# Three element-wise steps of an attention normalisation placed on GpSimd instead of two of them on VectorE, with another set of planner keys

## The chip, the cores and the metric

The kernel runs on one core of a Trainium2 chip. The metric is the device time of one execution in microseconds (us). Lower is better. Before the change three runs took 578.23, 578.06 and 575.93 us, a median of 578.06 us. The profiled execution is another one and took 579.15 us.

The engines are named as the profile names them: PE is TensorE's matmul, PEld its weight load, DVE is VectorE, ACT is ScalarE, POOL is GpSimd, SP is SyncE, which issues the DMAs.

## What is computed

A token-wise gate mixes two branches of the same input x (2048 tokens of 640 features):

```python
g = sigmoid((x * gate_w).sum(-1))
out = g * A(x) + (1 - g) * B(x)
```

Branch A is causal attention in four segments of 512 tokens with 32 heads of size 20, plus a linear memory that is carried from segment to segment. What is touched by the change is how its two parts are put together:

```python
for s in range(4):                                   # segments
    p = softmax(qs @ ks.T * scale + mask)
    a_dot = p @ vs
    num = phi(qs) @ M
    den = phi(qs) @ z + 1e-6
    a_mem = num / den
    o = g * a_mem + (1 - g) * a_dot                  # g = sigmoid(beta), one number for each head
    M, z = M + phi(ks).T @ vs, z + phi(ks).sum(rows)
```

The heads' outputs go through a 640x640 product with wo. Branch B picks the single token with the highest router score, sends it through a gated feed-forward net, and adds the result to that token alone.

## The kernel before

Work is cut into 32 groups n = 0 to 31, each of four heads of one segment. The heads are done in two halves; inside a half the segments s = 0 to 3 follow each other. For each of the eight (half, segment) units the kernel projects q, k and v on TensorE (each fp32 product as three passes on a high and a low part, line 704), writes the split q and k through DRAM and fetches them back in another layout, and then works through four groups.

One group has these steps. `a_step` (line 907) makes logits in five pieces on TensorE and VectorE reduces each to row maxima (lines 928 and 933). `maxima` (line 937) transposes these maxima and sends them into the rows of q by two small DMAs. `b_step` (line 960) makes the logits again, transposed, with the maximum taken off, ScalarE takes the exponential (line 975), and GpSimd zeroes the part above the diagonal (line 977). `pv_step` (line 983) multiplies by v (line 998); the v operand has a column of ones, so that the row sum of the softmax comes out as a 21st column. VectorE transposes that result into the first plane of a tile `nt` (line 1002). For segments 1 to 3, `memory_read` (line 845) has put phi(q) times the memory into the second plane of the same tile (lines 854 and 857), and GpSimd added 1e-6 to its denominators (line 859).

`norm` (line 1005) follows. VectorE takes the reciprocals of both denominators into a small tile `zr` (line 1012) and multiplies them by the gates (line 1013). It then multiplies the attention plane by its reciprocals (line 1017). Where s is above 0, GpSimd multiplies the memory plane by its own (line 1019) and VectorE adds the two planes (line 1020). Finally VectorE transposes the sum into a tile `on` (line 1021), of which there is only one, and a DMA writes it to DRAM. At the very end the heads' outputs are read back from DRAM, split into high and low parts (`o_load`, line 1195) and multiplied by wo (`o_job`, line 1216).

The order of all instructions on all engines is written out before the program is built, by a planner (`Plan.order`, line 207). Every task has an engine, an estimated duration, its dependences and a key. The planner steps through an imagined time, and at each step gives an engine the ready task with the lowest key. The keys are in units of one group: `n + PV` is the key of group n's last product, for example, and the constants at lines 51 to 69 set how far ahead of or behind its group each sort of task is wanted. The planner keeps two special rules: VectorE tasks that read two operands in SBUF (`lazy`) are not started while GpSimd is busy in the imagined time, and GpSimd tasks are not started while such a VectorE task runs (lines 246 to 249). Each engine then runs its list in that order, and waits where a dependence is not met.

A product that has been accumulated over one pair of row groups continues over the other pair only behind a "poke": VectorE copies two numbers out of the bank (line 692) and TensorE waits for that copy.

Of the kernel before, what the change touches and what calls it, by code (L numbers as in the profile page):

```python
# [14 lines left out]
OP = mybir.AluOpType  # L15
# [32 lines left out]
)  # L48
QTILE = {0: 0, 1: 1, 2: 3, 3: 4}
OFF = {0: 0, 1: 32, 2: 16, 3: 48}  # L50
LEAD = 3.1467
FIRST, UP, DOWN, DSTEP, FLOAD = 15.289, 0.1308, 19.6553, 0.2292, 0.944
LATER = 0.2501
PATIENCE = -0.3274
SHY = 2.468
EAGER = 1.4585
NEAR, FAR = 0.009, 0.0208
FETCH, XLOAD, XSPLIT = 1.3841, -0.8162, 1.0739
HALF, HSTEP, HLOAD, HALFV, HVSTEP = 0.0598, 0.099, 0.1226, 1.522, 0.1321
COPY, PHI, KEYS = 1.2662, 0.5548, 0.4812  # L60
MREAD, MWRITE, MSTEP = 0.7209, 1.594, 0.2955
PV, ASTEP, TOP, TURN, EXPS = 1.1417, 1.089, 0.738, 0.1362, 2.4648
WOAT, WOSTEP, OAT, OSTEP, OJOB, OLOAD = -0.4104, 0.1942, 0.9554, 0.0415, 0.1035, 0.4306
SLACK, GRACE = 0.1324, 0.1102
LASTO, LASTJ = 1.1526, 2.4243
WEIGHT = {"P1": 7.7099, "P2": 6.6659, "T4": 4.3409, "V0": 3.394, "V1": 7.0074}
PTS = 8
WARM = 13
POKE = 1.7235


ASTEPS = (([(0, 3, 0, 512)], 384, 1, 128), ([(0, 2, 0, 384), (0, 0, 384, 128)], 256, 2, 128),
# [14 lines left out]
def sub(ap, off, dims):  # L87
    return bass.AP(tensor=ap.tensor, offset=ap.offset + off, ap=[list(ap.ap[0])] + dims)
# [47 lines left out]
class Plan:  # L136
# [70 lines left out]
    def order(self):  # L207
# [24 lines left out]
        def choose(e):  # L232
# [44 lines left out]
            if e == "PE":  # L277
# [14 lines left out]
                def rank(c):  # L292
                    est, t = c
                    k = t.key
                    if t.opens is not None and t.opens.kind in DRAIN:
                        x = late[DRAIN[t.opens.kind]] - (est + t.dur + 0.3) - PATIENCE
                        k += SHY * x if x > 0 else EAGER * max(x, -1.0)
                    return k, t.seq
# [101 lines left out]
def tile_infini_mod(  # L400
# [12 lines left out]
    nc = tc.nc  # L413
# [27 lines left out]
    def dma(key, dst, src, reads, writes, desc, wide=16, issue=Plan.ISSUE, extra=0.0, kind="x"):  # L441
        kind = "in" if not reads else "out" if not writes else kind
        plan.add("SP", issue, lambda: nc.sync.dma_start(dst, src), key, reads, writes, desc=(*desc, wide, extra, kind))

    def dve(key, dur, fn, reads, writes, alone=None):
        n = sum(not isinstance(x[0] if isinstance(x, tuple) else x, Ps) for x in reads)
        plan.add("DVE", dur, fn, key, reads, writes, lazy=n > 1 and n == len(reads) if alone is None else alone)
# [4 lines left out]
    def pool(key, dur, fn, reads, writes):  # L452
        plan.add("POOL", dur, fn, key, reads, writes)

    def pe(key, dur, fn, reads, writes, mode="R", opens=None, lazy=False, fence=None):
        return plan.add("PE", dur, fn, key, reads, writes, mode=mode, opens=opens, lazy=lazy, fence=fence)
# [10 lines left out]
    def stream(n):  # L467
        return max(n * 0.000447 + 0.003, 0.11)
# [216 lines left out]
    def paired(ps, steps, operands, n, key_of, reads_of, kind):  # L685

        total, last, phase = len(steps), None, steps[0][1]
        for i, (k, ph) in enumerate(steps):
            fence = None
            if ph != phase:  # L690
                phase = ph
                poke = plan.add("DVE", 0.16, lambda: nc.vector.tensor_copy(nil.t, banks[ps.pair][0:1, :, 0:1]),  # L692
                                key_of(i) - POKE, poked=last)
                fence = (last, poke)
# [3 lines left out]
            def fn(i=i, k=k, ph=ph, ends=ends):  # L698
                t = banks[ps.pair]
                for p in range(3):  # L700
                    for r in range(2):
# [3 lines left out]
                                         start=i == 0 and p == 0, stop=ends and p == 2, skip_group_check=True)  # L705
            last = pe(key_of(i) + (LATER if kind != "O" else 0.0), 3 * stream(n) + 0.01, fn, reads_of(k), [ps], opens=ps if i == 0 else None, fence=fence)

# [275 lines left out]
    def pv_step(n, key):  # L983
        u, g = divmod(n, 4)
        ps = Ps("pv", 1)
        pos = (g + 2) % 4
        v = va[u % 2]
        assert now["v", u % 2, 0] == now["v", u % 2, 1] == u
        pt = {(p, c): pts.pop((n, p, c)) for p in range(2) for c in range(4)}

        def fn():
            o = banks[ps.pair]
            for c in range(4):
                w = L - 128 * c
                for j in range(4):
                    h = 4 * pos + j
                    t, to, pitch = pt[j % 2, c]
                    nc.tensor.matmul(o[32 * j:32 * j + 32, ps.bank, L - w:], v.t[:, c, VW * h:VW * h + 32],  # L998
                                     sub(t.t, 512 * (j // 2) + to, [[pitch, 4 - c], [1, 128]]), start=c == 0, stop=c == 3)
        pe(key, 2.2, fn, [*dict.fromkeys(t for t, *_ in pt.values()), v], [ps], mode="C", opens=ps)  # L1000
        nt = nts.pop(n) if n in nts else nt_ring.take()
        dve(key, 0.72, lambda: nc.vector.transpose(nt.t[:, 0, :], banks[ps.pair][:, ps.bank, :]), [ps], [(nt, 0)])  # L1002
        norm(n, nt, key)

    def norm(n, nt, key):

        u, g = divmod(n, 4)
        hf, s = divmod(u, SEG)
        z, o = zr_ring.take(), on_ring.take()
        i = 2 if s else 1  # L1010
        zz = z.t[:, :i, :]
        dve(key, 0.33, lambda: nc.vector.reciprocal(zz, sub(nt.t, DH, [[L, i], [32, 16]])), [(nt, a) for a in range(i)], [z])
        dve(key, 0.18, lambda: nc.vector.tensor_tensor(out=zz, in0=zz, in1=sub(gts.t, 2 * (4 * hf + g), [[1, i], [0, 16]]),
                                                       op=OP.mult), [z, gts], [z])
        dot, mem = (sub(nt.t, L * a, [[32, 16], [1, DH]]) for a in range(2))
        rd, rm = (sub(z.t, 16 * a, [[1, 16], [0, DH]]) for a in range(2))
        dve(key, 0.49, lambda: nc.vector.tensor_tensor(out=dot, in0=dot, in1=rd, op=OP.mult), [(nt, 0), z], [(nt, 0)])
        if s:
            pool(key, 0.73, lambda: nc.gpsimd.tensor_tensor(out=mem, in0=mem, in1=rm, op=OP.mult), [(nt, 1), z], [(nt, 1)])
            dve(key, 0.48, lambda: nc.vector.tensor_tensor(out=dot, in0=dot, in1=mem, op=OP.add), [(nt, 0), (nt, 1)], [(nt, 0)])  # L1020
        dve(key, 0.71, lambda: nc.vector.transpose(o.t, nt.t[:, 0, :]), [(nt, 0)], [o])
        h = HH * hf + 4 * g
        dma(key, oT[32 * h:32 * h + 128, L * s:L * s + L], o.t, [o], [oTb[n]], (128, 2048), kind="put")
# [217 lines left out]

    TOTAL = sum(WEIGHT.values())
    for u in range(NU):
        hf, s = divmod(u, SEG)
        base = 4 * u - LEAD if u else -5.0
        scale = 4.0 / TOTAL if u else (5.0 + 4 - LEAD) / TOTAL
        key = base
        for name in ("P1", "P2", "T4", "V0", "V1"):
            span = WEIGHT[name] * scale
            if name == "P1":  # L1250
# [13 lines left out]
        if u == SEG - 1:  # L1264
            kw = key - (WEIGHT["V0"] + WEIGHT["V1"]) * scale
            for i in range(2 * KT):
# [3 lines left out]
        if u == NU - 1:  # L1270
            kw = key - (WEIGHT["V0"] + WEIGHT["V1"]) * scale
            for k in range(KT):
# [72 lines left out]
```

## Time and profile before

| | |
|---|---|
| median of three runs | 578.06 us |
| profiled execution | 579.15 us |
| its span, first to last instruction | 577.1 us |
| TensorE matmul busy | 549.3 us, 95% |
| VectorE busy | 429.8 us, 74% |
| ScalarE busy | 354.7 us, 61% |
| GpSimd busy | 319.0 us, 55% |
| mean granted TensorE clock | 0.992 of full |

The busy times are unions over the span. An engine's idle time is put down to what released the instruction that ended it. A matmul's busy time is modelled at its end, so a fully busy TensorE may still be slowed inside; the idle times between its instructions are a lower bound of what it loses by waiting. On GpSimd an instruction's span is rough.

### The profile page before, as it was taken

To read this page: it belongs to the slowest core of one execution; us is meant where nothing else is said; L and a number is where in the kernel's file an instruction comes from. 1 tells how busy PE (TensorE), PEld (TensorE's weight loads), DVE (VectorE), ACT (ScalarE), POOL (GpSimd) and SP (SyncE) were. 2 spreads that over 40 slices of the span, in tenths; PEclk is the share of its full clock that TensorE was granted. 3 is DMA by queue.
4 is the path that set the end of the run, shared out by engine and by line. 5 is a ranking of instruction groups with operands and counts; after the bars stand their busy time and mean duration, and the time that the engine had idled before them with its cause. 6 is when DMAs were issued, how large, how long until landed. Compare 5 with 4: busy or idle time off the path is not lost.

```text
span 577.1 us, 18468 instructions
## 1 busy us (share of the span) xinstructions
PE 549.3 (95%) x7528; PEld 419.6 (73%) x7528; DVE 429.8 (74%) x736; ACT 354.7 (61%) x580; POOL 319.0 (55%) x399
## 2 busy tenths in 40 slices
PE   8999999999999999999999899998999898999996
PEld 4887867668668766786687566676668576788886
DVE  8757766668768878777796878678779978777653
ACT  6753866656548667777576657577666753545520
POOL 8872437425446667557564376468658643526330
PEclk9999999999999999999999979999999999999999
DMA  8787765547246856787597768785888566553722
GB/s 257 263 264 214 268 201 156 184 141 251 90 134 231 263 167 174 264 279 197 181 301 236 199 170 259 232 287 182 211 283 263 170 220 179 171 173 112 232 94 102
DMA packets 57685, 119.10 MB, mean 206 GB/s; under 512 B 6336, under 2 KB 13760, under 8 KB 57600
## 3 DMA queue, kind: packets, MB, share of 16 engines
q1 hardware_dynamic: 57600, 117.92, 64.3%
q8 instruction: 59, 0.97, 0.7%
q14 instruction: 26, 0.21, 0.1%
HBM read 72.28 MB, written 45.09 MB: 203 GB/s over the span
## 4 chain that ended last, share of the span: by engine, by line
PE 73%; DVE 13%; DMA 5%; issue 4%; ACT 3%; POOL 1%; POOLq 0%; SPq 0%; DVEq 0%; ACTq 0%
PE bank L704 39%; PE bank L998 11%; PE bank L918 6%; PE bank L971 6%; DVE mx L933 4%; PE bank L854 4%; PE bank L875 2%; PE bank L923 2%; DVE nt L1002 2%; ACT pt L975 1%; PE bank L836 1%; DVE nt L857 1%; DMA qs<-mr 1%; DMA ffn<-in_wg_dram 1%; DMA pt<-in_xT_dram 1%
## 5 line engine op out<-in xcount | busy, mean ns | idle before, releaser
L975 ACT ACTIVATE pt<-bank 128x1024 f32<-128x1024 f32 x160 | 160.3, 1024 | 103.6 <-PE bank L971 92.1
L933 DVE TENSOR_REDUCE mx<-bank 128x2 f32<-128x1024 f32 (+2 forms) x192 | 158.6, 861 | 28.2 <-PE bank L923 25.3
L977 POOL TENSOR_SCALAR_AFFINE_SELECT pt<-pt 128x512 f32<-128x512 f32 (+1 forms) x160 | 96.3, 604 | 113.6 <-ACT pt L975 105.6
L704 PE MATMUL bank<-xhi,whi 64*128 64x512 f32 (+1 forms) x460 | 94.4, 388 | 0.8 <-DVE nil L692 0.7
L704 PE MATMUL bank<-xlo,whi 64*128 64x512 f32 (+1 forms) x460 | 86.2, 353 | 0.0
L704 PE MATMUL bank<-xhi,wlo 64*128 64x512 f32 (+1 forms) x460 | 86.2, 352 | 0.0
L477 POOL TENSOR_TENSOR xlo<-raw,xhi 128x512 fp32r<-128x512 f32 x53 | 69.7, 1332 | 18.1 <-ACT xhi L473 9.6
L918 PE MATMUL bank<-ks,qs 60*128 60x256 f32 (+3 forms) x512 | 70.8, 326 | 6.4 <-DVE nt L857 1.5
L998 PE MATMUL bank<-pt,va 128*32 128x512 f32 (+3 forms) x1024 | 75.5, 435 | 1.0 <-DVE mt L884 0.6
L971 PE MATMUL bank<-qs,ks 62*128 62x256 f32 (+3 forms) x512 | 72.7, 349 | 3.8 <-DVE mx L933 2.0
L477 POOL TENSOR_TENSOR lo<-xs,hi 128x512 fp32r<-128x512 f32 x40 | 52.9, 1336 | 25.3 <-ACT hi L473 8.4
L998 PEld LDWEIGHTS bank<-pt,va 128*32 128x32 f32 x1024 | 30.9, 110 | 44.9 <-issue 36.4
L918 PEld LDWEIGHTS bank<-ks,qs 60*128 60x128 f32 x512 | 47.2, 188 | 19.7 <-DVE mx L933 3.4
L704 PE MATMUL bank<-vhi,xhi 64*128 64x322 f32 x320 | 59.2, 332 | 0.0
L971 PEld LDWEIGHTS bank<-qs,ks 62*128 62x128 f32 x512 | 45.0, 188 | 18.8 <-issue 7.3
L704 PE MATMUL bank<-vhi,xlo 64*128 64x322 f32 x320 | 55.3, 308 | 0.0
L704 PE MATMUL bank<-vlo,xhi 64*128 64x322 f32 x320 | 55.2, 308 | 0.0
L704 PEld LDWEIGHTS bank<-xhi,whi 64*128 64x128 f32 x460 | 49.0, 187 | 6.8 <-issue 1.7
L473 ACT CAST xhi<-raw 128x512 fp32r<-128x512 f32 x55 | 31.9, 618 | 35.4 <-DMA raw<-in_xT_dram 17.8
L704 PE MATMUL bank<-whi,xhi 64*128 64x320 f32 x320 | 52.0, 319 | 0.7 <-DVE nil L692 0.5
L704 PEld LDWEIGHTS bank<-xlo,whi 64*128 64x128 f32 x460 | 48.6, 186 | 5.5
L1002 DVE STREAM_TRANSPOSE nt<-bank 128x512 f32<-128x512 f32 x32 | 22.8, 713 | 39.7 <-PE bank L998 33.2
(148 smaller groups left out, 1158.9 us busy)
## 6 DMA issues: line engine op xcount, KB each, us to landing
stk<-hi SPq DMA_DIRECT2D x40, 512.0 KB
qs<-stk SPq DMA_DIRECT2D x64, 240.0 KB
ks<-stk SPq DMA_DIRECT2D x64, 240.0 KB
stk<-lo SPq DMA_DIRECT2D x40, 256.0 KB
raw<-in_xT_dram SPq DMA_DIRECT2D x35, 256.0 KB
oT<-on SPq DMA_DIRECT2D x32, 256.0 KB
ffn<-in_wd_dram SPq DMA_DIRECT2D x13, 320.0 KB
kk<-in_x_dram SPq DMA_DIRECT2D x12, 320.0 KB
```

Of the source, the lines that this page charges most:

```text
L473: act(key, acts(n) + 0.4 * more, lambda: nc.scalar.copy(hi, src), reads, [hpart])
L477: plan.add(engine, dur, lambda: e.tensor_tensor(out=lo, in0=src, in1=f32(hi), op=OP.subtract), key, [*reads, hpart], [lpart], lazy=engine ...
L704: nc.tensor.matmul(t[:, b, :n], w[64 * r:64 * r + 64], m[64 * r:64 * r + 64], start=i == 0 and p == 0, stop=ends and p == 2, skip_group_ch ...
L854: nc.tensor.matmul(t[32 * j:32 * j + 32, ps.bank, :], mbd.t[:, g, 32 * j:32 * j + 32], e.t, start=True, stop=True)
L875: nc.tensor.matmul(t[32 * m:32 * m + 32, ps.bank, :GW], kk.t[:, g, c, 32 * m:32 * m + 32], v.t[:, c, GW * pos:GW * pos + GW], start=c == 0 ...
L918: nc.tensor.matmul(a[:, b, to:to + w], q.t[64 * b:64 * b + ST, p, 128 * i:128 * i + 128], k.t[64 * b:64 * b + ST, p, :w], start=m == 0, st ...
L933: dve(key - TOP, 0.15 + 2 * w / 960.0, lambda p=p, i=i, to=to, w=w: nc.vector.tensor_reduce(out=sub(m_.t, 4 * p + i, [[8, 2], [1, 1]]), in ...
L971: nc.tensor.matmul(sub(bt, 512 * b + to, [[pitch, 4 - c], [1, 128]]), k.t[64 * b:64 * b + ST + 2, p, 128 * c:128 * c + 128], q.t[64 * b:64 ...
L975: act(key - EXPS, 0.22 + 2 * 512 / 1270.0, lambda: nc.scalar.activation(pt.t, banks[ps.pair], AF.Exp, scale=SCALE), [ps], [pt])
L977: pool(key, 0.42 if len(parts) == 1 else 0.64, lambda: nc.gpsimd.affine_select(out=d, in_=d, pattern=[[0, 2], [0, len(parts)], [1, 128]], ...
L998: nc.tensor.matmul(o[32 * j:32 * j + 32, ps.bank, L - w:], v.t[:, c, VW * h:VW * h + 32], sub(t.t, 512 * (j // 2) + to, [[pitch, 4 - c], [ ...
L1002: dve(key, 0.72, lambda: nc.vector.transpose(nt.t[:, 0, :], banks[ps.pair][:, ps.bank, :]), [ps], [(nt, 0)])
```

## The change

In `norm` two instructions change engine, and the memory product between them stays where it was. In segment 0 there is one product only; in the others the three GpSimd instructions of a group follow each other in GpSimd's own queue, with no return to VectorE between them. VectorE's transposition behind them (line 1021) then waits for GpSimd.

```diff
-        dve(key, 0.49, lambda: nc.vector.tensor_tensor(out=dot, in0=dot, in1=rd, op=OP.mult), [(nt, 0), z], [(nt, 0)])
+        pool(key, 0.73, lambda: nc.gpsimd.tensor_tensor(out=dot, in0=dot, in1=rd, op=OP.mult), [(nt, 0), z], [(nt, 0)])
         if s:
             pool(key, 0.73, lambda: nc.gpsimd.tensor_tensor(out=mem, in0=mem, in1=rm, op=OP.mult), [(nt, 1), z], [(nt, 1)])
-            dve(key, 0.48, lambda: nc.vector.tensor_tensor(out=dot, in0=dot, in1=mem, op=OP.add), [(nt, 0), (nt, 1)], [(nt, 0)])
+            pool(key, 0.73, lambda: nc.gpsimd.tensor_tensor(out=dot, in0=dot, in1=mem, op=OP.add), [(nt, 0), (nt, 1)], [(nt, 0)])
```

The planner's constants change too. All kinds and numbers of instructions that depend on them stay the same, apart from pokes, which the planner drops where it sees no need; the order on every engine and on the DMA queue is another one.

```diff
-LEAD = 3.1467
-FIRST, UP, DOWN, DSTEP, FLOAD = 15.289, 0.1308, 19.6553, 0.2292, 0.944
-LATER = 0.2501
-PATIENCE = -0.3274
+LEAD = 3.1128
+FIRST, UP, DOWN, DSTEP, FLOAD = 15.0716, 0.1213, 20.3681, 0.0113, 0.98
+LATER = 0.2788
+PATIENCE = -0.5118
...
-EAGER = 1.4585
+EAGER = 1.3294
...
-FETCH, XLOAD, XSPLIT = 1.3841, -0.8162, 1.0739
-HALF, HSTEP, HLOAD, HALFV, HVSTEP = 0.0598, 0.099, 0.1226, 1.522, 0.1321
-COPY, PHI, KEYS = 1.2662, 0.5548, 0.4812
-MREAD, MWRITE, MSTEP = 0.7209, 1.594, 0.2955
-PV, ASTEP, TOP, TURN, EXPS = 1.1417, 1.089, 0.738, 0.1362, 2.4648
-WOAT, WOSTEP, OAT, OSTEP, OJOB, OLOAD = -0.4104, 0.1942, 0.9554, 0.0415, 0.1035, 0.4306
-SLACK, GRACE = 0.1324, 0.1102
-LASTO, LASTJ = 1.1526, 2.4243
-WEIGHT = {"P1": 7.7099, "P2": 6.6659, "T4": 4.3409, "V0": 3.394, "V1": 7.0074}
+FETCH, XLOAD, XSPLIT = 1.4275, -0.7701, 1.062
+HALF, HSTEP, HLOAD, HALFV, HVSTEP = 0.1409, 0.08, -0.3718, 1.107, 0.1256
+COPY, PHI, KEYS = 1.2662, 0.4165, 0.5283
+MREAD, MWRITE, MSTEP = 0.5294, 1.594, 0.3187
+PV, ASTEP, TOP, TURN, EXPS = 1.1394, 1.089, 1.4258, 0.1735, 1.8485
+WOAT, WOSTEP, OAT, OSTEP, OJOB, OLOAD = -0.3432, 0.3005, 0.9854, 0.0452, 0.1035, 0.418
+SLACK, GRACE = 0.1324, 0.0853
+LASTO, LASTJ = 1.4126, 2.8484
+WEIGHT = {"P1": 7.8774, "P2": 6.7822, "T4": 4.4963, "V0": 2.6908, "V1": 7.189}
...
-POKE = 1.7235
+POKE = 2.3716
```

`TOP` is how much earlier than its group's key VectorE's row maxima are wanted, `EXPS` the same for the exponentials, `POKE` for the pokes, `HLOAD` for the loads of the second half's weights, `MREAD` for the reading of the memory. `DOWN` and `DSTEP` place the fourteen steps of the feed-forward net's last product, `LASTO` and `LASTJ` the last segment's read-back and product with wo.

## Rows read from the trace of the kernel before

**Rows 1.** The head of the page and the busy time of each engine, with its share of the span and its count of instructions.

```profile
span 577.1 us, 18468 instructions
PE 549.3 (95%) x7528; PEld 419.6 (73%) x7528; DVE 429.8 (74%) x736; ACT 354.7 (61%) x580; POOL 319.0 (55%) x399
```

**Rows 2.** The chain of work that ended last, its share of the span by engine.

```profile
PE 73%; DVE 13%; DMA 5%; issue 4%; ACT 3%; POOL 1%; POOLq 0%; SPq 0%; DVEq 0%; ACTq 0%
```

**Rows 3.** TensorE's matmul waits over the whole span, grouped by who was waited for: us in total, times, the longest. 34 lines, 22.1 us in all; 24 of them name VectorE and sum to 16.1 us, of which the first, some others, and the last stand here.

```profile
PE bank L971 <- DVE mx L933: 2.0, 3, 0.8
PE bank L918 <- DVE nt L857: 1.5, 1, 1.5
PE bank L725 <- POOL wlo L477: 1.4, 2, 1.0
PE bank L604 <- DVE pt L597: 1.3, 1, 1.3
...
PE bank L704 <- POOL xlo L477: 0.7, 1, 0.7
...
PE bank L875 <- DVE mbd L882: 0.2, 1, 0.2
```

**Rows 4.** Timeline of VectorE between 326 and 334 us: start, duration, instruction, and in brackets the idle time before it.

```profile
326.85 0.40 DVE L1013 TENSOR_TENSOR zr<-zr,gts 128x16 f32<-128x16 f32 x1
327.28 1.56 DVE L1017 TENSOR_TENSOR nt<-nt,zr 128x320 f32<-128x320 f32 x1
328.87 0.71 DVE L1021 STREAM_TRANSPOSE on<-nt 128x512 f32<-128x512 f32 x1
329.51 0.67 DVE L857 STREAM_TRANSPOSE nt<-bank 128x512 f32<-128x512 f32 x1
330.11 3.51 DVE L933 TENSOR_REDUCE mx<-bank 128x2 f32<-128x1024 f32 x4
```

**Rows 5.** Timeline of GpSimd in the same stretch.

```profile
327.19 1.30 POOL L477 TENSOR_TENSOR xlo<-raw,xhi 128x512 fp32r<-128x512 f32 x1
```

**Rows 6.** Timeline of TensorE's matmuls in the same stretch, the instructions that had idle time before them.

```profile
330.24 0.50 PE L918 MATMUL bank<-ks,qs 60*128 60x384 f32 x4 [1.53 <-DVE nt L857]
...
332.54 0.90 PE L971 MATMUL bank<-qs,ks 62*128 62x128 f32 x4 [0.62 <-DVE mx L933]
```

**Rows 7.** Busy time of each engine between 326 and 344 us, by stretches: the window, its length, PE, PEld, DVE, ACT and POOL busy, then the granted TensorE clock as a share of full speed, the DMA engines' share and GB/s.

```profile
326.00:328.00 2.00, 2.00 (x30) 1.81 (x30) 1.97 (x4) 1.60 (x3) 1.30 (x2) 1.00 0.63 175
328.00:330.00 2.00, 0.70 (x8) 0.23 (x4) 1.97 (x3) 0.76 (x2) 0.49 (x1) 1.00 0.98 203
330.00:332.00 2.00, 1.69 (x20) 1.17 (x20) 2.00 (x3) 2.00 (x5) 1.65 (x2) 1.00 0.80 266
332.00:334.00 2.00, 1.33 (x8) 0.91 (x10) 2.00 (x4) 0.73 (x2) 2.00 (x3) 0.56 0.57 149
334.00:336.00 2.00, 2.00 (x16) 1.63 (x16) 2.00 (x2) 1.17 (x3) 1.84 (x2) 0.50 0.61 185
336.00:338.00 2.00, 2.00 (x16) 1.66 (x12) 1.33 (x4) 1.44 (x2) 0.35 (x1) 0.50 0.79 214
338.00:340.00 2.00, 2.00 (x48) 1.60 (x44) 1.23 (x1) 1.26 (x2) 2.00 (x3) 0.73 0.37 131
340.00:344.00 4.00, 4.00 (x110) 2.76 (x110) 3.04 (x7) 2.82 (x5) 3.65 (x6) 1.00 0.49 148
```

**Rows 8.** Groups of instructions on VectorE and GpSimd: line, engine, operation, out<-in, count, then busy us and mean ns of one, then the idle time before them and its releasers.

```profile
L819 DVE SCALAR_TENSOR_TENSOR phi<-xs,phi 128x512 f32<-128x512 f32 x38 | 30.6, 814 | 4.3 <-ACT phi L818 4.2
...
L1017 DVE TENSOR_TENSOR nt<-nt,zr 128x320 f32<-128x320 f32 x32 | 17.0, 531 | 1.0
...
L1020 DVE TENSOR_TENSOR nt<-nt 128x320 f32<-128x320 f32 x24 | 15.1, 631 | 0.6 <-POOL nt L1019 0.6
L1019 POOL TENSOR_TENSOR nt<-nt,zr 128x320 f32<-128x320 f32 x24 | 23.6, 982 | 41.3 <-DVE zr L1013 40.8
```

**Rows 9.** The same lines taken one by one: count, then the shortest, the median and the longest instruction in ns, and the first and last start in us.

```profile
L1017 DVE TENSOR_TENSOR nt<-nt,zr x32: 475/492/1556, 77.0 to 553.4; 128x320 f32<-128x320 f32 x32
L1019 POOL TENSOR_TENSOR nt<-nt,zr x24: 730/1029/1040, 126.5 to 553.4; 128x320 f32<-128x320 f32 x24
L1020 DVE TENSOR_TENSOR nt<-nt x24: 468/484/1265, 128.5 to 555.2; 128x320 f32<-128x320 f32 x24
L819 DVE SCALAR_TENSOR_TENSOR phi<-xs,phi x38: 648/681/1993, 25.2 to 451.8; 128x512 f32<-128x512 f32 x38
```

**Rows 10.** Timelines of VectorE and GpSimd around two of the memory products: at 126 us, where the attention product runs beside it, and at 199 us, where it is over.

```profile
126.47 0.49 DVE L1017 TENSOR_TENSOR nt<-nt,zr 128x320 f32<-128x320 f32 x1
126.53 1.03 POOL L1019 TENSOR_TENSOR nt<-nt,zr 128x320 f32<-128x320 f32 x1
198.46 0.49 DVE L1017 TENSOR_TENSOR nt<-nt,zr 128x320 f32<-128x320 f32 x1
199.22 0.73 POOL L1019 TENSOR_TENSOR nt<-nt,zr 128x320 f32<-128x320 f32 x1
```

**Rows 11.** Waits over the whole span, all engines: us in total, times, the longest.

```profile
POOL pt L977 <- ACT pt L975: 105.6, 87, 4.4
...
POOL nt L1019 <- DVE zr L1013: 40.8, 16, 7.2
...
ACT pt L975 <- POOL pt L977: 3.7, 4, 1.6
```

**Rows 12.** The stretch of 16 us among those behind the start in which GpSimd was busiest (columns as in rows 7).

```profile
432.00:448.00 16.00, 14.80 (x238) 12.73 (x238) 15.07 (x22) 10.56 (x18) 13.41 (x11) 1.00 0.80 260
```

**Rows 13.** The end of the kernel: two timelines of VectorE (the last group's add and the last split of its read-back) and the longest piece of the chain that ended last, in TensorE's product with wo.

```profile
555.17 0.87 DVE L1020 TENSOR_TENSOR nt<-nt 128x320 f32<-128x320 f32 x1
564.88 0.69 DVE L477 TENSOR_TENSOR xlo<-raw,xhi 128x512 fp32r<-128x512 f32 x1 [2.63 <-ACT xhi L473]
555.74 14.26 PE bank L704 x188
```

## The prediction

> **What bounds the kernel.** Start with the busy times [rows 1]. TensorE works 549.3 of 577.1 us, so nothing that leaves its work alone can win more than its idle 27.8 us and what a lowered clock costs it. The change removes no matmul. VectorE is second at 429.8 us. The chain that ended last agrees: TensorE holds 73% of it, VectorE 13%, GpSimd 1% [rows 2]. So the question is which of TensorE's idle time hangs on VectorE. The waits of the matmuls say so [rows 3]: 24 of 34 lines name VectorE, 16.1 of 22.1 us. They are spread thin: the largest line has 2.0 us. They come from VectorE's queue as a whole, mostly from banks that it empties late, and not from `norm`, which no TensorE instruction reads. GpSimd's lines are small (1.4 and 0.7 us are its largest). `norm` can reach TensorE only by keeping VectorE from something else.
>
> One place shows that in full. At 327.19 GpSimd starts a split of 1.30 us [rows 5]. At 327.28 VectorE comes to the attention product, which reads two SBUF operands and takes 1.56 us [rows 4] where the median is 0.49 [rows 9]; it ends 0.35 us after the split does. The transposition of the memory's result sits behind it in VectorE's queue [rows 4], TensorE waits 1.53 us for its bank, and 0.62 us more for a reduction [rows 6]. Then the granted clock drops: it is 0.56, 0.50, 0.50 and 0.73 of full in the four stretches from 332 to 340 us, that is 1.2 in place of 2.4 GHz, after two stretches in which TensorE worked 0.70 and 1.69 of 2.00 us [rows 7]. The loss is 2 x (0.44 + 0.50 + 0.50 + 0.27) = 3.4 us. One stalled product cost about 1.5 + 3.4 = 4.9 us, ten times its normal length.
>
> **The change part by part.** *Off VectorE:* 32 attention products, 17.0 us, and 24 additions, 15.1 us [rows 8], together 32.1 us. Its busy time falls from 429.8 to 397.7 us, 69% of the span.
>
> *Onto GpSimd:* 56 instructions of the memory product's shape. That takes 0.73 us after the attention product is over and 1.03 beside it [rows 10]. I take 0.73 (also the shortest [rows 9]): the product that ran beside it goes to GpSimd itself, and most of what VectorE then runs is reductions and transpositions out of PSUM. 56 x 0.73 = 40.9 us; the other end is 56 x 1.03 = 57.7. The 24 memory products lose their neighbour: 23.6 - 24 x 0.73 = 6.1 us come back [rows 8]. GpSimd goes from 319.0 to about 354 us (61%), at most 377.
>
> *The wait.* The attention product waits on GpSimd for the reciprocals, as the memory product does now; for that GpSimd already stands 40.8 us in 16 waits [rows 11]. New is segment 0, where GpSimd had no part in `norm` (8 groups). Behind the waiting instruction are the zeroing of exponentials and the low parts of splits. The zeroing has 105.6 us of idle time in 87 waits for ScalarE ahead of it [rows 11], which hides a few us spread over the kernel; without it, the price is that of the third rival. VectorE's last transposition waits for GpSimd's add, as the add itself waits for GpSimd's product now, which cost VectorE 0.6 us in all [rows 8]. What queues behind it are reductions that free TensorE's banks. The three steps in a row take 3 x 0.73 = 2.2 us, against 1.03 + 0.48 = 1.5 us now. I charge 1.0 us for such waits (bounds 0 and 0.7 x 24 = 17 us, the low end because the planner puts other work between, and the row of 0.6 us is the nearest).
>
> *What the lighter VectorE gives TensorE.* First the stretch at 327 us. The product that stalled is no longer on VectorE. I count 1.53 us of wait and 3.4 us of clock as gone: -4.9 us. Bounds: 0, if another stall takes its place, and 5.6 with the second wait. Then the other VectorE waits: 16.1 less 1.3 at the start (a memset ahead of the first matmul [rows 3]) less 1.5 counted above leaves 13.3 us. How much goes when VectorE has 7% less work isn't shown by any row; nothing and all 13.3 are the bounds, and a loss isn't excluded, since the order is another one. My estimate treats them as a queue's waits, growing with busy over idle time: 429.8/147.3 = 2.92 now, 397.7/179.4 = 2.22 then, a quarter less: -3.3 us.
>
> *Locks the other way.* VectorE's remaining instructions with two SBUF operands can now run into 35 us more of GpSimd work. The phi step is the row to go by: mean 814 against a shortest 648 ns, 38 times [rows 8, 9], so 6.3 us lost against 319 us of GpSimd; scaled, 0.7 us more, perhaps 1.5 with the other such instructions, on VectorE and not on TensorE. I take nothing for it and keep it as a rival. On this the Trainium skill (SBUF — State Buffer, "Who interferes with whom") is harsher: a VectorE instruction with two SBUF inputs and a GpSimd instruction that reads SBUF exclude each other, and the second one is blocked for the whole of the first. The product of 1.56 us behind the split agrees; the memory product, 0.06 us behind VectorE's 0.49, is lengthened by 0.30 us [rows 10], not by the 0.43 that are left, so it is not quite a full block. By that rule the sum would stay as it is, and the chance of the second rival's mechanism rises.
>
> *The end.* The last group's add ends at 556.04 now, because GpSimd and an output step held it up; three GpSimd steps from 553.4 end at about 555.6. Were it 1.2 us late, it is covered: TensorE multiplies without a gap from 555.74 for 14.26 us, while the last split is done at 565.57 [rows 13]. Without that cover it costs up to 1.2 us. I take 0.
>
> *The other keys.* They reorder every queue: VectorE's maxima and pokes come earlier in rank, exponentials later, the second half's weights are loaded later on SP's queue ahead of their splits, and the steps of the last feed-forward product bunch. No row gives a price. The gain is bounded by TensorE's waits for others than VectorE, 22.1 - 16.1 = 6.0 us; the loss by one more event like that at 327 us, 4.9. I take 0, being between them.
>
> **The sum.** 579.15 (profiled) - 4.9 - 3.3 + 1.0 = 571.95 us. The median of the runs is 1.09 below the profiled one: 570.9, so 571 us, 1.2% less than 578.06. Its own range is 563 to 575: 8 us better if the keys give 6.0 and a few more of VectorE's waits go, 4 worse if the waits stay.
>
> **Rivals.** *Nothing to be measured.* VectorE's relief lies in idle time, and the stall at 327 us turns up elsewhere, since a drop of the clock needs only one bad place. For it: VectorE already idles 147 us. Against it: its waits lead TensorE's list. Then only 0 to 3.3 us less 1.0 are left: 576 to 579, say 577.
>
> *Slower by the shared access.* The added GpSimd work catches VectorE's two-operand steps in two or more places as the split caught the product at 327 us, with the clock dropping after each. The place is where the splits, phi and the feed-forward steps meet (320 to 450 us). For it: phi's longest is 1.99 us [rows 9], so such catches happen. Against it: the moved instructions were themselves the victims. Price 4.9 us each: with one such event the clock term is as it was; it is slower from two on: 579.15 + 4.9 - 1.09 = 583 with VectorE's quarter lost.
>
> *Slower by GpSimd's queue.* Zeroing comes behind three products, `pv_step` waits and TensorE with it. For it: one stretch has GpSimd busy 13.41 of 16 us [rows 12]. Against it: the average is 55%, and ScalarE waited for a zeroed buffer just 3.7 us [rows 11]. If every second group's last product comes one GpSimd step late, 16 x 0.73 = 11.7 us: 570.9 + 11.7 = 583. It decides from the eleventh such group on (11 x 0.73 = 8.0).
>
> **How the numbers follow.** Forecast 0.56, nothing 0.20, shared access 0.13, GpSimd's queue 0.11. A measurement of this kernel can tell about 0.5%, that is 2.9 us. Faster is below 575.2: 0.56. Same: 0.20. Slower, above 580.9: 0.24. The range has to reach over the middle case and into the slower ones: 562 to 583 us leaves out some 0.05 below and about half of the slower cases.
>
> **What would show it.** Right: attention product and add on GpSimd near 730 ns, the memory product's mean down from 982 towards 750; VectorE near 398 and GpSimd near 354 us; VectorE's lines among TensorE's waits down from 16.1 to about 11 us; no stretch with the clock at half. Wrong: a clock drop behind another VectorE stall (first and second rival), phi's mean above 814 ns (second), or the zeroing among TensorE's waits with several us (third). The size fails if TensorE's busy time itself moves by more than the 3.4 us of the clock, since no step here gives a reason for that.

## The result and the profile after

Slower by 0.6%: the median of 20 runs is 582.93 us (579.18 to 584.81), beside 578.30 us (575.49 to 581.57) for 20 runs of the kernel before. The ratio (after to before) is 1.006, 95% interval 1.0042 to 1.0077. The forecast was 571 us and faster; the time lies just inside the range of 562 to 583 us, on the side that had a chance of 0.24. The means further down leave out three slow runs, one each of the kernel before, of the repetition of after and of after_no_gx.

The page of the changed kernel, its head and busy times, to be held against [rows 1]:

```profile
span 581.9 us, 18464 instructions
...
PE 553.0 (95%) x7528; PEld 419.4 (72%) x7528; DVE 404.9 (70%) x683; ACT 355.3 (61%) x580; POOL 357.7 (61%) x455
```

The move did what it says. VectorE's busy time fell by 24.9 us, and GpSimd's rose by 38.7 us (forecast: 32.1 and 35). TensorE is the row to look at. Its busy time rose by 3.7 us and its idle time by 1.1 us, from 27.8 to 28.9; that is the whole 4.8 us by which the span is longer. TensorE's matmuls are the same 7528, so 3.7 us more of busy time for them means a slower engine and not more work.

Where it was slower is in the busy times by stretches (the columns of [rows 7]: PE, PEld, DVE, ACT and POOL busy, then the granted clock):

```profile
208.00:210.00 2.00, 2.00 (x56) 1.08 (x44) 1.68 (x4) 0.45 (x3) 1.28 (x1) 1.00 0.71 227
210.00:212.00 2.00, 0.75 (x8) 0.30 (x6) 1.93 (x5) 1.82 (x3) 0.70 (x2) 1.00 1.03 218
212.00:214.00 2.00, 1.34 (x18) 1.12 (x16) 1.87 (x4) 0.42 (x1) 1.92 (x4) 0.83 0.61 180
214.00:216.00 2.00, 1.43 (x32) 0.96 (x34) 2.00 (x4) 2.00 (x7) 1.83 (x4) 0.50 0.36 136
216.00:218.00 2.00, 2.00 (x28) 0.57 (x18) 0.70 (x1) 0.54 (x3) 0.87 (x2) 0.50 0.28 70
218.00:220.00 2.00, 2.00 (x14) 1.48 (x12) 1.52 (x4) 1.14 (x2) 1.20 (x3) 0.50 0.07 20
...
464.00:466.00 2.00, 1.42 (x20) 0.82 (x16) 2.00 (x3) 1.32 (x2) 1.92 (x3) 1.00 0.83 213
466.00:468.00 2.00, 1.50 (x16) 0.84 (x16) 2.00 (x3) 0.98 (x2) 0.64 (x1) 1.00 0.77 135
468.00:470.00 2.00, 1.03 (x12) 0.67 (x10) 2.00 (x4) 2.00 (x4) 1.08 (x2) 0.83 0.65 221
470.00:472.00 2.00, 1.69 (x8) 0.20 (x8) 1.57 (x3) 2.00 (x5) 2.00 (x3) 0.50 0.70 242
472.00:474.00 2.00, 2.00 (x16) 0.90 (x16) 1.39 (x2) 0.69 (x1) 1.25 (x3) 0.50 0.67 247
474.00:476.00 2.00, 2.00 (x16) 0.69 (x12) 1.43 (x3) 0.00 (x0) 0.75 (x1) 0.50 0.66 223
```

The drop at 332 us [rows 7] is gone, as forecast. In its place there are two: the clock goes to 1.2 GHz at 213 and again at 469 us, each time behind stretches in which TensorE was busy 0.75 to 1.50 of 2.00 us. Each costs about 3.4 us (2 x 0.17 + 3 x 1.0, and the rest just behind), so the profiled run of after loses 6.8 us to the clock and that of before 3.4. Elsewhere in this trace TensorE was nearly as thin and the clock stayed (4.5 of 6.00 us busy from 410 to 416), so a thin stretch does not always bring a drop.

TensorE's waits over the whole span, against [rows 3], the longest lines by who was waited for (us, times, the longest):

```profile
PE bank L918 <- ACT pt L975: 2.5, 3, 1.5
PE bank L971 <- DVE mx L933: 1.5, 4, 0.6
PE bank L918 <- DVE mt L884: 1.5, 2, 1.3
PE bank L918 <- DVE mx L933: 1.4, 3, 0.8
```

All 30 lines sum to 23.0 us (22.1 before), the 21 of VectorE to 15.0 (16.1), those of ScalarE to 5.9 (3.1). With a lighter VectorE and another order its lines are 1.1 us shorter in sum, and ScalarE's grew by more.

### The profile page after: what moved, and what is told of

Same layout as the page of the kernel before. It is cut to its first block, busy times and chain, and to the rows that moved or that the text cites. A ratio compares the mean times of both kernels' runs of the same rounds, so it can differ in the third digit from the quotient of the medians.

```text
span 581.9 us, 18464 instructions
## 1 busy us (share of the span) xinstructions
PE 553.0 (95%) x7528; PEld 419.4 (72%) x7528; DVE 404.9 (70%) x683; ACT 355.3 (61%) x580; POOL 357.7 (61%) x455
## 4 chain that ended last, share of the span: by engine, by line
PE 74%; DVE 10%; DMA 9%; issue 3%; ACT 2%; POOL 1%; SPq 1%; DVEq 0%; POOLq 0%; ACTq 0%
PE bank L704 41%; PE bank L998 10%; PE bank L918 6%; PE bank L971 6%; PE bank L854 4%; DMA raw<-in_xT_dram 3%; DVE mx L933 3%; PE bank L875 3%; PE bank L923 2%; DVE nt L1002 2%; ACT pt L975 2%; DMA ffn<-in_wd_dram 1%; DMA qs<-stk 1%; DMA qs<-mr 1%; DMA ffn<-in_wg_dram 1%
## 5 line engine op out<-in xcount | busy, mean ns | idle before, releaser
L933 DVE TENSOR_REDUCE mx<-bank 128x2 f32<-128x1024 f32 (+2 forms) x192 | 159.6, 862 | 40.8 <-PE bank L923 37.5
L998 PE MATMUL bank<-pt,va 128*32 128x512 f32 (+3 forms) x1024 | 76.9, 441 | 0.5 <-ACT va L776 0.3
L1017 POOL TENSOR_TENSOR nt<-nt,zr 128x320 f32<-128x320 f32 x32 | 26.1, 816 | 61.3 <-DVE zr L1013 55.8
L704 PE MATMUL bank<-vhi,xhi 64*128 64x322 f32 x320 | 57.6, 338 | 0.5 <-DVE nt L1002 0.3
L704 PE MATMUL bank<-vhi,xlo 64*128 64x322 f32 x320 | 52.6, 307 | 0.0
L704 PE MATMUL bank<-vlo,xhi 64*128 64x322 f32 x320 | 52.6, 307 | 0.0
```

The source lines that it names most:

```text
L704: nc.tensor.matmul(t[:, b, :n], w[64 * r:64 * r + 64], m[64 * r:64 * r + 64], start=i == 0 and p == 0, stop=ends and p == 2, skip_group_ch ...
L933: dve(key - TOP, 0.15 + 2 * w / 960.0, lambda p=p, i=i, to=to, w=w: nc.vector.tensor_reduce(out=sub(m_.t, 4 * p + i, [[8, 2], [1, 1]]), in ...
L1017: pool(key, 0.73, lambda: nc.gpsimd.tensor_tensor(out=dot, in0=dot, in1=rd, op=OP.mult), [(nt, 0), z], [(nt, 0)])
```

## The experiments

Two sizes are needed to read them. Every run has its time and its mean granted clock. Time x mean clock is about what it would have taken at full clock; the rest I call the clock's loss. The split is rough. The mean also covers the last few us, where TensorE is done, and from run to run of before 1 us of loss goes with only 0.5 us of time (in after with 1.0). The means have standard errors of 0.2 to 1.1 us, the larger ones where there are only 6 or 8 runs. Differences of about 1 us in the last two columns are not safe. In the list of all kernels the order is that of before or of after, taken over unchanged, or "re-planned", when the planner made a new one. The kernel before stands for its runs beside the experiments, after for its 20 runs and those of its repetition.

```
kernel           order        runs  mean us  mean clock  time x clock  loss
before           before         85    579.3      0.9958         576.9   2.4
before_without   before         12    576.6      0.9960         574.3   2.3
move_frozen      before         10    583.7      0.9970         582.0   1.8
after            after          31    582.0      0.9898         576.0   5.9
after_without    after          12    580.8      0.9891         574.4   6.3
unmove_frozen    after           6    587.9      0.9875         580.5   7.4
after_no_gx      after          11    582.9      0.9895         576.8   6.1
after_fill       after           8    584.4      0.9877         577.2   7.2
after_open       after          12    581.0      0.9937         577.3   3.7
after_open_ctl   after          12    582.7      0.9878         575.5   7.1
after_open_both  after           6    574.8      0.9975         573.3   1.4
move_only        re-planned      6    586.4      0.9847         577.4   9.0
keys_only        re-planned      6    604.3      0.9742         588.6  15.6
```

**One half of the change at a time.** First the move under the old keys, and the new keys without the move.

```diff
# move_only: constants of before, and
-        dve(key, 0.49, lambda: nc.vector.tensor_tensor(out=dot, in0=dot, in1=rd, ...
+        pool(key, 0.73, lambda: nc.gpsimd.tensor_tensor(out=dot, in0=dot, in1=rd, ...
-            dve(key, 0.48, lambda: nc.vector.tensor_tensor(out=dot, in0=dot, in1=mem, ...
+            pool(key, 0.73, lambda: nc.gpsimd.tensor_tensor(out=dot, in0=dot, in1=mem, ...
# keys_only: the reverse of these lines, with the constants of after
```

> The three products of norm on GpSimd, with the planner's constants of before (the planner orders all queues anew for it). Theory K, the new keys cost the time and the move by itself helps or is free: 572 to 578 us, ratio 0.99 to 1.00 of before. Rival M, the move costs the time (GpSimd's queue or the shared access): 582 to 585 us, ratio about 1.007, with the clock at half twice and TensorE waiting for the zeroing or for VectorE steps behind GpSimd. Rival O, any new order shifts where TensorE runs thin, and the time follows the number of clock drops at 3.4 us each: VectorE's busy time falls to about 400 us and the time does not follow it; anything from 575 to 585.

> The planner's constants of after, with the attention product and the addition on VectorE as before. Theory K: as slow as after or slower, 582 to 588 us. Rival M: as fast as before, 576 to 579 us. Rival O: anything from 575 to 588, VectorE back near 430 us, and the time told by the count of clock drops and not by VectorE's load.

Measured: move_only 586.05 us, ratio 1.0108 (1.0066 to 1.015); keys_only 604.64 us, ratio 1.0431 (1.0396 to 1.0466). Neither K (the keys cost it, the move is free) nor M (the move costs it) holds: each half is slower than both together. Rival O (any new order shifts where TensorE runs thin) fits move_only in kind: its time x clock is near that of before and after, 577.4 us, and it loses 9.0 us to the clock, with three drops in the profiled run; the time is 1 us above O's range. O does not cover keys_only, the worst in both sizes: it is 16.6 us above O's upper end, and 11.7 us of what it loses against before stands at full clock, where TensorE's waits sum to 33.3 us (22.1 in before). A new plan is made whenever a task changes its engine or a constant changes, and keys that fit one plan do not fit another, so re-planned kernels can't tell the two halves apart. That asks for kernels with the order held fixed.

**The move without a new order.** Here the planner is told what it was told before, and only the emitted instruction goes to the other engine.

```diff
# move_frozen: the order of before
-        dve(key, 0.49, lambda: nc.vector.tensor_tensor(out=dot, ...
+        dve(key, 0.49, lambda: nc.gpsimd.tensor_tensor(out=dot, ...
# (the addition likewise; unmove_frozen: the order of after, pool(...) tasks that issue nc.vector)
```

> The order of before, exactly as its planner wrote it out, TensorE's, ScalarE's and the DMA queue's lists unchanged; the 56 instructions are only issued on GpSimd, at the place in time where VectorE had them. If a lighter VectorE helps TensorE where the order is the same: VectorE near 398 us, no stall like that at 327 us, 570 to 575 us. If GpSimd's queue or the transposition behind three GpSimd steps costs more than is won: 580 us and above. If VectorE's load lies in idle time and only the clock drops tell: 576 to 579, with VectorE's waits in TensorE's list near 16 us as before.

> The order of after, with the attention product and the addition issued on VectorE in the place in time where GpSimd had them; TensorE's, ScalarE's and the DMA queue's lists unchanged. If the move cost the time: 576 to 579 us. If the move helps and the order of after costs it: 586 to 592 us. If the load is of no weight: 581 to 584 us, as after.

Measured: move_frozen 582.77 us, ratio 1.0064 (1.0036 to 1.0091); unmove_frozen 587.93 us, ratio 1.0149 (1.011 to 1.0188). Move_frozen loses hardly anything to the clock (1.8 us), and is 5.1 us longer at full clock. Its group of the last transposition says why (busy us, mean ns, then the idle time before it and its releasers):

```profile
L1021 DVE STREAM_TRANSPOSE on<-nt 128x512 f32<-128x512 f32 x32 | 22.7, 710 | 33.2 <-POOL nt L1020 28.1 <-POOL nt L1017 5.1
```

VectorE is 27.7 us less busy there (402.1 us) and stands 33.2 us waiting for GpSimd: the wait takes the place of the work, with the reductions queued behind it. TensorE's waits sum to 27.2 us, 5.1 more than in before. In after the planner has put other work in between, and the same group shows 2.9 us:

```profile
L819 DVE SCALAR_TENSOR_TENSOR phi<-xs,phi 128x512 f32<-128x512 f32 x38 | 31.9, 848 | 3.4 <-ACT phi L818 3.3
...
L1017 POOL TENSOR_TENSOR nt<-nt,zr 128x320 f32<-128x320 f32 x32 | 26.1, 816 | 61.3 <-DVE zr L1013 55.8 <-DVE nil L692 5.0
...
L1021 DVE STREAM_TRANSPOSE on<-nt 128x512 f32<-128x512 f32 x32 | 22.4, 701 | 2.9 <-POOL nt L1020 2.0 <-POOL nt L1017 0.8
...
L1020 POOL TENSOR_TENSOR nt<-nt 128x320 f32<-128x320 f32 x24 | 21.8, 908 | 1.8
...
L1019 POOL TENSOR_TENSOR nt<-nt,zr 128x320 f32<-128x320 f32 x24 | 20.2, 841 | 0.0
```

So the move alone costs 5.1 us at full clock in an order that doesn't expect it, most likely by this wait (no kernel takes the wait away alone), and that is not what after pays. Undoing the move in the order of after is no better: +4.5 us at full clock, with TensorE's waits for VectorE at 19.6 us, where after has 15.0. Its time lies where a move that helps was expected, but a step that is put on another engine than the planned one costs about as much in either direction, so these two kernels can't price the move.

**What the 56 instructions are worth.** They are left out on either engine, in each of the two orders; the rest of the lists stays.

```diff
# before_without: the order of before; after_without: the order of after
-        ... lambda: nc.vector.tensor_tensor(out=dot, in0=dot, in1=rd, op=OP.mult), ...
+        ... lambda: None, ...
# (the addition likewise; in after it is nc.gpsimd that goes)
```

> The order of before with the 32 attention products and 24 additions left out altogether, on either engine (the output lacks them): the most that a lighter VectorE can give in that order, with nothing put on GpSimd and no wait for it. The forecast's step (the stall at 327 us gone for 4.9 us, a quarter of VectorE's other waits for 3.3 us) expects 569 to 572 us. If VectorE's load lies in idle time and TensorE's idle time comes from the order and from latencies: at most 1 to 3 us less than before, 576 to 578 us, VectorE near 398 us and TensorE's waits for it still above 13 us.

> The order of after with the same 56 instructions left out (on GpSimd only the memory product remains; the output lacks the rest). If they cost the time of after, on GpSimd or by locking VectorE out: 575 to 579 us, GpSimd near 309 us. If the time of after is that of its order and of its clock drops: 580 to 583 us, with mean clocks near 0.989 as before.

Measured: before_without 576.06 us, ratio 0.996 (0.9935 to 0.9986); after_without 580.26 us, ratio 1.003 (1.0002 to 1.0057). This is the test on which the forecast falls. With the 32 us gone from VectorE and nothing put anywhere else, the order of before gains 2.7 us of time (576.6 for 579.3), 2.6 of it at full clock and nothing at the clock (loss 2.3 for 2.4 us), where the forecast had 8.2 us. Its busy times:

```profile
PE 546.4 (95%) x7528; PEld 417.2 (72%) x7528; DVE 397.8 (69%) x680; ACT 356.1 (62%) x580; POOL 309.5 (54%) x399
```

VectorE is where the forecast wanted it. TensorE's lines for VectorE still sum to 14.4 us, and its lines for all engines to 23.9 (22.1 in before), since those of ScalarE grew from 3.1 to 5.3. The two orders without these steps are alike at full clock, 574.3 and 574.4 us; with them they are at 576.9 (on VectorE) and 576.0 us (on GpSimd). So the steps cost about 2.6 us on VectorE and 1.6 us on GpSimd. The 1.0 us between these is not clear of noise (its standard error is about 0.6), so it is not shown that the move is worth anything. The plain means say the same without the split: without the steps the order of after is 4.2 us longer than that of before (580.8 and 576.6); the steps add 1.2 us on GpSimd to the one and 2.7 us on VectorE to the other. What makes after slower is its order, and that stands in the last column: the order of before loses about 2 us to the clock with or without the steps, the order of after about 6.

**Why the order of after loses more.** At 213 us it looked like the forecast's second rival. GpSimd's split and a small VectorE step for the token gate, which took 0.19 us in the kernel before:

```profile
208.18 1.28 POOL L477 TENSOR_TENSOR xlo<-raw,xhi 128x512 fp32r<-128x512 f32 x1 [0.92 <-ACT xhi L473]
...
208.25 1.24 DVE L1076 TENSOR_SCALAR gx<-gx 128x16 f32<-128x16 f32 x1 [1.39 <-ACT gx L1075]
```

The step began 0.07 us behind the split and ended 0.03 us after it. Two kernels went for this place, one without the step, one with idle matmuls ahead of TensorE's wait.

```diff
# after_no_gx
-        dve(key, 0.2, lambda: nc.vector.tensor_scalar(gx.t, gx.t, 1.0, None, op0=OP.add), [gx], [gx])
+        dve(key, 0.2, lambda: None, [gx], [gx])
# after_fill
+    for i, t in enumerate(plan.order()):
+        if i == 1241:
+            for _ in range(5):
+                nc.tensor.matmul(banks[0][:, 1, :], tri.t[64:128, :], sub(id64.t[64:128], 0, [[0, 8], [1, 64]]), ...)
```

> The order of after with one small VectorE instruction left out: the addition of 1 to the token gate (128x16, line 1076), which took 1.24 us at 208.25 us because a split of GpSimd held it up, just before TensorE ran thin and the clock fell at 213 us. If a caught VectorE step makes the drop: the first drop goes in most runs, mean clock up by about 0.006, 3 to 4 us less than after, 578 to 580 us. If the stretch is thin anyway (VectorE waits there for ScalarE, and banks come free late): as after, 582 to 583 us.

> The order of after with five idle matmuls of 512 bf16 columns (about 0.21 us each) put into TensorE's queue ahead of the one that waited 1.25 us at 210 us; nothing else is changed. If the thin stretch makes the clock fall: drop at 213 us gone in most runs, mean clock up by about 0.006, 2 to 4 us less than after, 579 to 581 us. If one full gap is not enough, or the drop comes from elsewhere: 582 to 584 us, at most 1 us more than after.

Measured: after_no_gx 583.49 us, ratio 1.0066 (1.0038 to 1.0093), loss 6.1 us; after_fill 583.12 us, ratio 1.0088 (1.0053 to 1.0123), loss 7.2 us. The caught step is not the cause: without it the clock still falls at the same place, where TensorE's stretch is still thin (1.39, 1.43 and 1.02 of 2.00 us from 210 to 216 us). In unmove_frozen the same step is caught (1.25 us), the stretch is thin (1.45, 1.25 and 1.36 us), and the clock of the profiled run stays at 1.00 there. Ahead of the second drop no VectorE step was caught at all: from 462 to 471 us the trace of after has reductions, a transposition and two small steps, none of them long. The filler does not settle it, because its matmuls, on line 1306 of that kernel, had themselves to wait for a bank:

```profile
PE bank L1306 <- DVE nt L857: 1.4, 1, 1.4
```

That wait names what is short in these stretches: TensorE stands until VectorE or ScalarE has read a bank of PSUM, the memory that its products go to. So in the next kernels banks come free without being read.

```diff
     for t in plan.order():
+        if 199.0 <= t.start < 214.0 or 444.0 <= t.start < 456.5:      # the planner's imagined time
+            if any((t.eng, p.kind) in (("DVE", "a"), ("ACT", "b")) for p in t.ps):
+                continue
         t.fn()
# after_open: only ("DVE", "a"), 201 to 212 and 446 to 454.5; after_open_ctl: the same, 166 to 187 and 412 to 428
# shown: after_open_both
```

> The order of after with 13 of VectorE's 224 reductions to row maxima left out, those in the two stretches ahead of its drops of the clock (about 204 to 215 and 461 to 471 us), so that their banks come free at once; the maxima of these groups are not computed. TensorE's, ScalarE's and the DMA queue's lists are unchanged. If the drops come from these thin stretches: they go, the clock's loss falls from 6 us (mean clock 0.989) to 2 us or less (0.996), and with some 2 to 4 us of TensorE's waits there the time is 573 to 577 us. If they come from elsewhere or from the phase of the run: only the waits go, 579 to 581 us, mean clock still near 0.989.

> The control: the order of after with 17 reductions left out in two other stretches of it (about 168 to 190 and 425 to 444 us), in which the clock did not fall; the maxima of these groups are not computed. If VectorE's load as such were what counts: as much faster as the kernel with the 13 left out. If the thin stretches ahead of the drops are what counts: 581 to 583 us, mean clock near 0.989.

> The order of after with 17 reductions of VectorE and 10 exponentials of ScalarE left out in the two stretches ahead of its drops (about 202 to 217 and 460 to 472 us), since with the reductions alone gone TensorE waited there for ScalarE's banks instead; the results of these groups are not computed. TensorE's, GpSimd's and the DMA queue's lists are unchanged. If thin stretches make the drops and these are the two: TensorE's wait there goes (some 4 us) and the clock's loss with it, mean clock 0.995 or more, 572 to 576 us. If the clock does not depend on them: only the waits, 578 to 580 us, mean clock near 0.989.

> The kernel after once more, as it is, beside the kernel before on the same chip: 582 to 584 us, mean clock near 0.989 and the kernel before near 0.995, if the loss belongs to the order and not to the chip of the first measurement; 578 to 580 us and equal clocks otherwise.

Measured: after_open 581.56 us, ratio 1.002 (0.999 to 1.0051); the control after_open_ctl 582.47 us, 1.0062 (1.0032 to 1.0091); after_open_both 574.87 us, 0.99 (0.987 to 0.993); after_again 582.28 us, 1.0039 (1.0009 to 1.007). With the reductions alone gone, the clock's loss fell only from 5.9 to 3.7 us, between the two that were expected, and the time stayed at the upper one. TensorE then waited for ScalarE instead (9.1 us in all, 5.9 in after), and the first stretch stayed thin and lost the clock:

```profile
210.00:212.00 2.00, 1.28 (x14) 0.76 (x16) 1.58 (x6) 2.00 (x3) 1.05 (x2) 1.00 0.97 197
212.00:214.00 2.00, 1.44 (x18) 0.82 (x16) 1.08 (x3) 0.29 (x2) 1.92 (x4) 1.00 0.99 268
214.00:216.00 2.00, 0.65 (x20) 0.65 (x24) 0.04 (x1) 2.00 (x6) 1.83 (x4) 0.84 0.45 165
...
466.00:468.00 2.00, 1.18 (x18) 0.78 (x18) 0.87 (x2) 1.02 (x1) 1.77 (x3) 1.00 0.50 128
468.00:470.00 2.00, 1.19 (x20) 0.86 (x16) 0.00 (x0) 1.86 (x3) 0.43 (x1) 1.00 0.81 167
470.00:472.00 2.00, 1.82 (x19) 0.57 (x16) 0.71 (x1) 2.00 (x4) 1.53 (x2) 1.00 0.77 269
```

The second stretch was hardly fuller than in after, and its clock held in this run; another drop, of 1.7 us, came at 341 us, behind 2 us in which TensorE was busy 0.49. So which thin stretch loses the clock is not settled by these busy times alone.

With the exponentials gone as well both are filled (after_open_both), and the clock holds there:

```profile
210.00:212.00 2.00, 1.67 (x22) 0.97 (x20) 1.58 (x6) 1.26 (x2) 1.16 (x2) 1.00 0.99 212
212.00:214.00 2.00, 1.55 (x34) 1.04 (x34) 1.02 (x3) 0.47 (x1) 1.92 (x4) 1.00 0.91 263
214.00:216.00 2.00, 2.00 (x44) 1.09 (x37) 0.50 (x2) 1.77 (x8) 1.84 (x4) 1.00 0.40 142
...
466.00:468.00 2.00, 2.00 (x24) 0.84 (x24) 0.50 (x3) 0.99 (x3) 2.00 (x3) 1.00 0.64 132
468.00:470.00 2.00, 1.63 (x24) 0.74 (x24) 1.46 (x2) 1.08 (x2) 2.00 (x3) 1.00 0.80 260
470.00:472.00 2.00, 2.00 (x39) 1.55 (x30) 0.92 (x2) 1.21 (x2) 1.83 (x3) 1.00 0.52 172
```

The loss is then 1.4 us in the mean of six runs (mean clock 0.9975), and the time 7.2 us below after's mean: 4.5 us of it from the clock, 2.7 at full clock. Even so the profiled run, the slowest of the six, lost 1.7 us in a drop at 381 us, behind 2 us in which TensorE was busy 0.19. The control took as many reductions away (17, where after_open took 13), in stretches where the clock had not fallen, and kept its loss (7.1 us). The greater loss of after therefore comes from these two stretches: filling them removes it, and lightening VectorE elsewhere doesn't. One gap is left, since no kernel leaves out exponentials elsewhere. And the loss belongs to the order, not to the chip of the first measurement, since the repetition beside the kernel before shows the same clocks as the first 20 runs.

## Why the prediction was wrong

*The step that failed* is "what the lighter VectorE gives TensorE", the 8.2 us on which the forecast rested, in both of its terms: with the order held fixed, before_without gives 2.6 us in their place.

The first term took one drop of the clock as a consequence of one stalled product (-4.9 us), and so as gone with it. The stall went, and the drop at 332 us with it, but the loss came back larger at two other places: 2.4 us on average before, 5.9 after. In the order of before, taking the product away changes the average loss by 0.1 us (before_without), though the profiled run of that kernel has no drop. The profiled run of before showed one drop of 3.4 us; by their mean clocks (1.000 to 0.989) the runs of that kernel lose from nothing to some 6 us. So the sum took off the clock's loss of one run as if every run had it. It then took off another 1.09 us for the distance of the median from that run, which may be partly the same loss: by its mean clock of 0.992 the profiled run lost 4.6 us, 2.2 more than the average. The loss goes with the whole order, and not with the step that happened to be late in the profiled run; how much of it one run loses differs, and no run here shows what decides which thin stretch loses the clock.

The second term took TensorE's waits for VectorE as a queue's, to shrink with the load (-3.3 us). Measured, all of the load taken away gives 2.6 us at full clock, both terms together; the waits for VectorE went from 16.1 to 14.4 us. Much of the time that VectorE was given it spent waiting for TensorE in its turn. Ahead of the 192 reductions of line 933 it stood 25.3 us for TensorE's logits in before and 39.7 in before_without, in the same order; in after it was 37.5 (the rows in this order):

```profile
L933 DVE TENSOR_REDUCE mx<-bank 128x2 f32<-128x1024 f32 (+2 forms) x192 | 158.6, 861 | 28.2 <-PE bank L923 25.3
L933 DVE TENSOR_REDUCE mx<-bank 128x2 f32<-128x1024 f32 (+2 forms) x192 | 158.7, 862 | 42.6 <-PE bank L923 39.7
L933 DVE TENSOR_REDUCE mx<-bank 128x2 f32<-128x1024 f32 (+2 forms) x192 | 159.6, 862 | 40.8 <-PE bank L923 37.5
```

So 14.4 of the 32 us went into a longer wait. That the banks which TensorE still waits for could not have been emptied sooner fits this, but no kernel here tested it.

*The other keys* were taken at 0, with a loss bounded by one more event of 4.9 us. The bounds held: without the moved steps the order of after is 4.2 us longer, and all of after has 3.5 us more loss at the clock and 0.9 us less at full clock. But the sign of the whole result sits in this term, and it had been given the least thought, since no row priced it. Which constant makes the two stretches thinner was not tried, nor whether the keys or the move itself gave the planner this order; the drops of move_only and keys_only come mostly at other places again.

*Off VectorE* came out 7.2 us short (404.9 for 397.7 us). In the order of before leaving the steps out gives 397.8 us, in that of after 402.8, so 5.0 us of it go with the order. *Onto GpSimd* was right in kind and somewhat small in size: 68.1 us for the three groups (816, 841 and 908 ns) where 730 ns each would be 58. *Locks the other way*: phi's mean went from 814 to 848 ns, 1.3 us in all, as estimated (0.7 to 1.5).

*The wait* was charged at 1.0 us, and VectorE stood 2.9 us for GpSimd before its last transposition. The bound above it is what an unexpecting order pays: 33.2 us of VectorE, 5.1 us of the kernel (move_frozen).

*The rivals.* The second named the time (583 us) and partly the way: two drops of the clock. Its mechanism was there once, the caught step at 208 us, but leaving that step out changed nothing (583.49 us, loss 6.1 us), and ahead of the second drop there was no catch; so it isn't the cause, and the time is met by luck. The third is excluded: none of TensorE's 30 lines names the zeroing, and GpSimd's one line there is 1.2 us. What GpSimd's queue costs shows only in the 1.6 us at full clock that the steps cost on GpSimd (576.0 against 574.4), no more than the 2.6 us that they cost on VectorE. The first rival was nearest in what it said of VectorE: its relief lies in idle time, and the drop turns up elsewhere. But its time (576 to 579 us) allowed for one drop and not for two.

*On the shared access* the Trainium skill (SBUF — State Buffer, "Who interferes with whom") also says that a VectorE tensor_scalar can enter a mode that takes the port which GpSimd uses, though it reads one operand. The trace of after agrees: line 1076, one small operand, 1.24 us behind a split where it took 0.19 before.

## What to carry to other kernels

Before you count a gain for unloading an engine that others wait for, leave the work out altogether, with the order held fixed: here 32 us less of VectorE were worth 2.6 us, and in that order no other place for the work can be expected to win more. Where the order is planned, split a result into time at full clock and the clock's loss, over several runs; a loss seen in one profiled run isn't won by removing the stall in front of it, unless the stretch is filled. And a step moved to another engine without a new plan turns into a wait there: test placement and order apart, and judge them together.

## What the runs showed of the hardware

The clock's loss varies from run to run of one program: the 20 runs of after range from a mean clock of 0.996 with 580.04 us to 0.983 with 584.81 us. The clock did not fall behind every thin stretch: in unmove_frozen TensorE was busy 4.06 of the 6 us from 210 us on and kept 2.4 GHz, in after 3.52 of the same 6 us and lost it. A VectorE step with a single operand of 128x16 was held up by GpSimd for as long as one with two operands: 1.24 us for 0.19, beside 1.56 for 0.49 (line 1017 at 327 us in before).
